# Attention followed by channel mixing: the on-chip decoding of weight pieces, spread differently over three engines

## The chip, the cores and the metric

The kernel runs on one core of a Trainium2 chip. The core has a matrix engine (TensorE, in the profile PE, with its weight loads as PEld), three engines for elementwise work (VectorE or DVE, ScalarE or ACT, GpSimd or POOL), and SyncE (SP), which here issues nearly all transfers. Each engine works through its own instructions in order. The metric is the device time of one execution in microseconds (us). Before the change it is 1101.88 us, the median of 3 runs (1100.26 to 1106.89).

## The reference

The first part is linear attention with random features, for 8 batches of 8 heads, 576 rows and 64 columns; the second is a mixing along the rows by a product of low rank and then a two-layer network over the 512 channels.

```python
def phi(x):                                  # q and k scaled first
    h = np.einsum('bhsd,md->bhsm', x, omega) - np.sum(x * x, axis=-1, keepdims=True) / 2.0
    return np.exp(h - np.max(h, axis=-1, keepdims=True)) / np.sqrt(m)
kv = np.einsum('bhsm,bhsd->bhmd', phi(k), v)
num = np.einsum('bhsm,bhmd->bhsd', phi(q), kv)
den = np.einsum('bhsm,bhm->bhs', phi(q), np.sum(phi(k), axis=2))[..., None] + 1e-06
x = (num / den)                              # heads side by side: 8 x 576 x 512
...
h = x.transpose(0, 2, 1) @ U @ V             # U 576 x 32, V 32 x 576
u = x + h.transpose(0, 2, 1)
out = u + np.maximum(u @ w_ch1, 0.0) @ w_ch2 # w_ch1 512 x 2048, w_ch2 2048 x 512
```

q, k, v and omega are fp32. U, V, w_ch1 and w_ch2 come in fp64, which the chip has no arithmetic for: the kernel reads each number as two 32-bit words and builds an fp32 number from them. fp32 products are made on TensorE from a high and a low part of each operand.

## The kernel before, in words

**Attention.** 16 units (a pair of heads each, keys or queries of them) of 9 tiles of 128 rows make 144 steps; the loop at L761 to L843 writes them out with fixed delays between the stages of one step (the table `DELAY`). A step's chain is: load of kt or qt (SP, L531), transposition xT (VectorE, L551), high part xh (ScalarE, L555), low part xl (GpSimd, L559), the projection p_p (TensorE, three products, L678 to L680), the negative maximum nm over its features (VectorE, L686), four exponentials e, one for each 128x128 quarter (ScalarE, L693), and then, for keys, p_kv (TensorE, L590), and for queries a transposition p_q (TensorE, L616), its copy eT (ScalarE or VectorE, L621), the product p_n (TensorE, L636) and the division into x (VectorE, L661). "Exp step 30" below means the four exponentials of the thirtieth step.

**Mixing.** As soon as a pair of batches has its x, a generator (`mixing`, 4 pairs, 9 tiles each) makes a high part mh (ScalarE, L347) and a low part ml (L349) of each 128x512 tile of x, multiplies them by U and V, and stores u. The low part is made on GpSimd, and on VectorE for the last pair.

**Decoding.** In two of three steps the loop advances the generator `decoding` by one slot. A piece is 128x512 numbers of a weight. It is loaded as 128x1024 words (SP, L183) into one of two raw buffers. For the first 11 pieces (U, two of V, eight of w_ch1, `EARLY`), the ones that the attention loop finishes, the work is: absolute value of the high word as a float (ScalarE, L132); on VectorE a clamp to two bounds (L150), a shift (L151), the merge of the sign from the raw high word (L154), a mask that keeps the exponent (L157) and the low word times that exponent (L158), which is the last to read the raw buffer; and on GpSimd one addition (L172). These are five slots, one VectorE step each. Pieces after that have three slots: for them ScalarE also casts the low word to an integer (L135) and the addition is one of integers. The ScalarE steps of the next piece are written in the fourth slot (third for later pieces), and the next load in the last.

**What sets the order.** The instructions are handed to a scheduler that simulates the engines with costs of its own and orders each engine's instructions by that; those wrapped in `K`, that is `tc.keep_in_program_order`, keep the order in which they are written. SP issues its transfers in the order that results, and a transfer into a buffer that is still in use holds up all transfers behind it.

After attention comes an opening, then the up phase (`unit`, L855, products L891) and the down phase (L1181, L1200); the remaining pieces are decoded there.

## Time and profile before

| | before |
|---|---|
| median of 3 runs | 1101.88 us |
| the profiled execution | 1101.12 us, span 1099.3 us |
| mean granted TensorE clock | 0.979 |
| PE, PEld busy | 95%, 93% of the span |
| DVE, ACT, POOL busy | 78%, 55%, 47% |
| the attention loop | about the first 325 us |

A row of the windows view gives a stretch of the execution, its length, the busy time of each engine with the number of its instructions, and the granted clock. A row of the waits view names an engine and a line that stood idle and what ended that idleness: total, times, longest. A row of the timeline gives start, length, engine, line and operation, and in brackets the idle time ahead of it with what ended it. A row of the groups view gives count, total busy time, mean of one in ns, and after the bar the idle time before them.

### The profile page before, as it was taken

How to read it: one execution, taken by the hardware profiler on the slowest of the kernel's cores; microseconds unless marked ns; L12 is line 12 of the kernel's file. 1: busy time of each engine (PE TensorE's matmuls, PEld its weight loads, DVE VectorE, ACT ScalarE, POOL GpSimd, SP SyncE). 2: the span in 40 equal slices, each digit the busy share in tenths (PEclk: the TensorE clock that was granted, in tenths of full speed). 3: DMA queues.
4: the chain of work that ended last, by engine and by line, in shares of the span. 5: the costliest groups of instructions: out<-in, count | busy, mean ns of one | idle time of the engine just before them, and what ended most of it. 6: DMA issues, size and time to landing. Idle time of an engine off the chain costs nothing. (4 is left out here: it accounts for less than half of the span.)

```text
span 1099.3 us, 23900 instructions
## 1 busy us (share of the span) xinstructions
PE 1049.2 (95%) x8497; PEld 1023.6 (93%) x8497; DVE 857.2 (78%) x1550; ACT 601.1 (55%) x1471; POOL 520.9 (47%) x451
## 2 busy tenths in 40 slices
PE   8999988999997899999999999989999999999998
PEld 7998878899996899899999999979999999999998
DVE  3787998898898778766665555778888888888886
ACT  4877978889873555555453344554443443344433
POOL 3445976956433534313312102545456455564563
PEclk8898999999997999999999999999999999999999
DMA  7778577576434686778778743544544444444442
GB/s 129 138 143 168 96 175 154 104 181 120 92 87 102 200 226 133 193 208 215 212 192 213 202 124 107 164 121 154 172 159 145 168 159 144 165 162 172 156 144 97
DMA packets 382199, 170.31 MB, mean 155 GB/s; under 512 B 283488, under 2 KB 357216, under 8 KB 377472
## 3 DMA queue, kind: packets, MB, share of 16 engines
q1 hardware_dynamic: 382016, 168.72, 58.5%
q8 instruction: 67, 1.10, 0.4%
q14 instruction: 52, 0.43, 0.1%
q0 software_dynamic: 64, 0.07, 0.0%
HBM read 107.91 MB, written 60.82 MB: 153 GB/s over the span
## 5 line engine op out<-in xcount | busy, mean ns | idle before, releaser
L1054 ACT CAST gh<-gs 128x512 fp32r<-128x512 f32 x140 | 83.2, 619 | 208.1 <-DVE gs L1028 161.0
L693 ACT ACTIVATE e<-p_p,nm 128x128 f32<-128x128 f32 x576 | 166.8, 389 | 27.6 <-DVE nm L686 20.5
L1028 POOL TENSOR_TENSOR gs<-graw 128x512 f32<-128x512 f32 x70 | 113.3, 1639 | 110.9 <-DMA graw<-g 79.4
L559 POOL TENSOR_TENSOR xl<-xT,xh 128x384 fp32r<-128x384 f32 x96 | 101.6, 1076 | 116.9 <-ACT xh L555 92.9
L875 ACT ACTIVATE g<-g 128x512 f32<-128x512 f32 x108 | 67.8, 631 | 161.2 <-DVE g L879 116.8
L1055 DVE TENSOR_TENSOR gl<-gs,gh 128x512 fp32r<-128x512 f32 x140 | 112.5, 815 | 53.5 <-ACT gh L1054 53.5
L686 DVE TENSOR_REDUCE nm<-p_p 128x4 f32<-128x512 f32 x144 | 98.1, 682 | 28.5 <-PE p_p L680 14.8
L1126 POOL TENSOR_TENSOR u<-u,p 128x256 f32<-128x256 f32 x72 | 80.4, 1146 | 55.4 <-DVE u L1126 54.2
L678 PE MATMUL p_p<-omh,xh 128*128 128x256 f32 x288 | 94.6, 329 | 2.3 <-ACT e L693 2.2
L172 POOL TENSOR_TENSOR wf<-wf,low 128x512 int32<-128x512 int32 x24 | 32.1, 1337 | 113.2 <-ACT g L875 59.9
L636 PE MATMUL p_n<-kv,eT 128*128 128x65 f32 x512 | 76.3, 278 | 7.6 <-ACT eT L621 3.4
L680 PE MATMUL p_p<-omh,xl 128*128 128x256 f32 x288 | 83.1, 289 | 0.0
L679 PE MATMUL p_p<-oml,xh 128*128 128x256 f32 x288 | 82.6, 287 | 0.0
L891 PE MATMUL p_n<-uh,wh 128*128 128x256 f32 x272 | 78.6, 289 | 3.9 <-DVE g L879 3.9
L636 PEld LDWEIGHTS p_n<-kv,eT 128*128 128x128 f32 x512 | 70.1, 199 | 13.0 <-DVE eT L621 4.0
L1200 PE MATMUL p_p<-wh,gh 128*128 128x256 f32 x288 | 81.1, 282 | 0.0
L1200 PE MATMUL p_p<-wh,gl 128*128 128x256 f32 x288 | 81.0, 281 | 0.0
L1200 PE MATMUL p_p<-wl,gh 128*128 128x256 f32 x288 | 80.9, 281 | 0.0
L1055 DVE TENSOR_TENSOR gl<-graw,gh 128x512 fp32r<-128x512 f32 x107 | 75.2, 730 | 4.4 <-ACT gh L1054 4.4
L1200 PE MATMUL p_q<-wh,gl 128*128 128x256 f32 x276 | 77.8, 282 | 0.7 <-DVE gl L1055 0.6
L891 PE MATMUL p_n<-uh,wl 128*128 128x256 f32 x272 | 78.2, 287 | 0.0
L891 PE MATMUL p_n<-ul,wh 128*128 128x256 f32 x272 | 78.1, 287 | 0.0
(246 smaller groups left out, 4055.6 us busy)
## 6 DMA issues: line engine op xcount, KB each, us to landing
g<-g SPq DMA_DIRECT2D x288, 128.0 KB, 2.4
graw<-g SPq DMA_DIRECT2D x36, 1024.0 KB, 5.0
raw<-in_moe_w_ch_dram SPq DMA_DIRECT2D x22, 512.0 KB, 4.7
u_dram<-ut SPq DMA_DIRECT2D x36, 256.0 KB, 2.4
uraw<-u_dram SPq DMA_DIRECT2D x144, 64.0 KB, 2.6
u<-u_dram SPq DMA_DIRECT2D x36, 256.0 KB, 2.6
out_dram<-u SPq DMA_DIRECT2D x36, 256.0 KB, 2.2
kt<-in_k_dram SPq DMA_DIRECT2D x120, 72.0 KB, 2.6
```

The source lines that it names most:

```text
L559: nc.gpsimd.tensor_tensor(out=self.xl[-1], in0=self.turned, in1=f32(self.xh[-1]), op=ALU.subtract)
L636: nc.tensor.matmul(pn[:, h, :], eT[:, h, :], kv[:, h, s // 5, :], start=True, stop=True)
L678: nc.tensor.matmul(o, part.xh[g][:, ts], oh, start=True, stop=False)
L679: nc.tensor.matmul(o, part.xh[g][:, ts], ol, start=False, stop=False)
L680: nc.tensor.matmul(o, part.xl[g][:, ts], oh, start=False, stop=True)
L686: nc.vector.tensor_reduce(out=self.nm[:, :n], in_=self.pp[:, :n], axis=AX.X, op=ALU.max, negate=True)
L693: nc.scalar.activation(out=self.e[:, j, :], in_=self.pp[:, j, :], func=AF.Exp, bias=self.nm[:, j : j + 1])
L891: K(nc.tensor.matmul(p[:, f, :], x[:, k, fs], y[:, k, :], start=first, stop=(k == 1 and y is ul), skip_group_check=True,))
L1028: K(engine.tensor_tensor(out=to, in0=self.val[x], in1=self.val[y], op=op))
L1054: K(nc.scalar.copy(out=h, in_=v))
L1055: K(nc.vector.tensor_tensor(out=l, in0=v, in1=f32(h), op=ALU.subtract))
L1200: K(nc.tensor.matmul(acc[bank][:, half, :], x[:, ks], y[:, f, :], start=(now.s == 0 and k == 0 and half == 0 and x is h and y is wh), stop ...
```

## The change

All pieces are now decoded as the later ones were: ScalarE casts the low word (L134 in the new numbering, directly behind the absolute value, L132) and GpSimd adds integers (L166), so the mask and the low word's product leave VectorE. For the first 11 pieces the clamp moves from VectorE to GpSimd as well (L139), so VectorE has a shift (L150) and a sign merge (L153) left. The slots of these pieces remain five, with work in the second and the third only. GpSimd's addition and the next load are written in the third slot, since the sign merge is now the last reader of the raw high word; the ScalarE steps of the next piece are written in the fifth. In the mixing, the low parts of odd tiles go to VectorE for the first three pairs too: 12 of their 27.

```diff
         def magnitude(i):
             if i < len(jobs):
-                mags[i] = jobs[i][2]()
-                nc.scalar.activation(out=mags[i], in_=f32(raws[i][:, :, 1]), func=AF.Abs)
-                if i >= lean:
-                    lows[i] = dec.tile([P, PIECE], I32, name="low", tag="de", bufs=2)[:, : jobs[i][1]]
-                    nc.scalar.activation(out=lows[i], in_=raws[i][:, :, 0], func=AF.Copy, scale=2.0**-29)
+                m = mags[i] = jobs[i][2]()
+                nc.scalar.activation(out=m, in_=f32(raws[i][:, :, 1]), func=AF.Abs)
+                lows[i] = dec.tile([P, PIECE], I32, name="low", bufs=2)[:, : jobs[i][1]]
+                nc.scalar.activation(out=lows[i], in_=raws[i][:, :, 0], func=AF.Copy, scale=2.0**-29)
+                if i < early:
+                    bound(nc.gpsimd, m)
+
+        def bound(engine, m):
+            return engine.tensor_scalar(m, m, _LEAST, _MOST, ALU.max, ALU.min)
...
             slots = [
-                lambda: nc.vector.tensor_scalar(m, m, _LEAST, _MOST, ALU.max, ALU.min),
+                lambda: bound(nc.vector, m),
...
-                lambda: nc.vector.tensor_scalar(words(e), words(m), 0xFF800000, None, ALU.bitwise_and),
-                lambda: nc.vector.scalar_tensor_tensor(e, low, 2.0**-52, e, ALU.mult, ALU.mult),
             ]
-            if i >= lean:
-                slots = slots[:3]
+            if i < early:
+                slots = [lambda: None, *slots[1:], lambda: None, lambda: None]
             for j, slot in enumerate(slots):
-                tc.keep_in_program_order(slot())
+                op = slot()
+                if op is not None:
+                    K(op)
                 for _ in range(-(-len(rest) // (len(slots) - j))):
                     rest.pop(0)()
-                if j == (len(slots) - 1 if i >= lean else 3):
+                if j == 2:
+                    K(nc.gpsimd.tensor_tensor(out=m.bitcast(I32), in0=m.bitcast(I32), in1=low, op=ALU.add))
+                    fetch(i + 1 + depth())
+                if j == len(slots) - 1:
                     magnitude(i + 1)
-                if j == len(slots) - 1:
-                    fetch(i + 1 + depth())
                 yield
-            whole = (lambda ap: ap.bitcast(I32)) if i >= lean else (lambda ap: ap)
-            nc.gpsimd.tensor_tensor(out=whole(m), in0=whole(m), in1=e, op=ALU.add)
             rest = [lambda fn=fn, m=m: fn(m) for fn in job[3:]]
...
-                rest = nc.vector if last else nc.gpsimd
+                rest = nc.vector if last or t % 2 else nc.gpsimd
                 rest.tensor_tensor(out=xl, in0=x[:, t, :], in1=f32(xh), op=ALU.subtract)
```

The scheduler's order is changed in the whole attention loop. Two places show how. The first is SP's queue around the loads of the fifth and the sixth piece (both of w_ch1); vt and vm are loads of v, kt and qt those of k and q. Before:

```order
L531 DMA kt_976<-in_k_dram 32x18x32 x8
L531 DMA qt_1014<-in_q_dram 32x18x32 x8
L573 DMA vt1_122<-in_v_dram 128x4x64 x2
L577 DMA vm1_123<-in_v_dram 64x2x64
L183 DMA raw_1123<-in_moe_w_ch1_dram 128x1024
L573 DMA vt1_122<-in_v_dram 128x4x64 x2
L577 DMA vm1_123<-in_v_dram 64x2x64
L531 DMA kt_1288<-in_k_dram 32x18x32 x8
L531 DMA qt_1326<-in_q_dram 32x18x32 x8
L183 DMA raw_1372<-in_moe_w_ch1_dram 128x1024
```

The same stretch of SP's queue after the change, where these two loads are raw_1024 and raw_1259:

```order
L529 DMA kt_975<-in_k_dram 32x18x32 x8
L529 DMA qt_1013<-in_q_dram 32x18x32 x8
L181 DMA raw_1024<-in_moe_w_ch1_dram 128x1024
L571 DMA vt1_122<-in_v_dram 128x4x64 x2
L575 DMA vm1_123<-in_v_dram 64x2x64
L571 DMA vt1_122<-in_v_dram 128x4x64 x2
L575 DMA vm1_123<-in_v_dram 64x2x64
L529 DMA kt_1289<-in_k_dram 32x18x32 x4
L181 DMA raw_1259<-in_moe_w_ch1_dram 128x1024
L529 DMA kt_1289<-in_k_dram 32x18x32 x4
L529 DMA qt_1327<-in_q_dram 32x18x32 x8
```

The fifth load has moved ahead of three transfers, two of vt and one of vm; the sixth ahead of twelve, four of kt and eight of qt. In the same way the third load (the second piece of V) has moved ahead of three transfers and the fourth (the first of w_ch1) ahead of six.

The second place is ScalarE where it first reads the fifth piece, between exp steps 30 and 33 (e_1189, e_1222, e_1254 and e_1284). Before:

```order
L693 ACTIVATE e_1189<-p_p_1146,nm_1187 128x128 x4
L621 COPY eT_1194<-p_q_1175 128x256
L322 CAST svm_119<-sv_118 128x64
L555 CAST xh_1206<-xT_1192 128x384
L555 CAST xh_1236<-xT_1196 128x384
L693 ACTIVATE e_1222<-p_p_1178,nm_1220 128x128 x4
L693 ACTIVATE e_1254<-p_p_1211,nm_1252 128x128 x4
L621 COPY eT_1260<-p_q_1240 128x256
L693 ACTIVATE e_1284<-p_p_1243,nm_1282 128x128 x4
L132 ACTIVATE wf_1059<-raw_1123 128x512
L555 CAST xh_1307<-xT_1297 128x384
```

The same exp steps on ScalarE after the change (e_1187, e_1220, e_1252 and e_1285):

```order
L691 ACTIVATE e_1187<-p_p_1147,nm_1185 128x128 x2
L553 CAST xh_1204<-xT_1190 128x384
L132 ACTIVATE wf_1121<-raw_1024 128x512
L134 ACTIVATE low_1371<-raw_1024 128x512
L553 CAST xh_1234<-xT_1194 128x384
L691 ACTIVATE e_1220<-p_p_1176,nm_1218 128x128 x4
L691 ACTIVATE e_1252<-p_p_1209,nm_1250 128x128 x4
L619 COPY eT_1261<-p_q_1238 128x256
L691 ACTIVATE e_1285<-p_p_1241,nm_1283 128x128 x4
L553 CAST xh_1308<-xT_1298 128x384
L132 ACTIVATE wf_1652<-raw_1259 128x512
```

ScalarE's first reading of the fifth piece has moved from behind exp step 33 to behind exp step 30, and behind exp step 33 it now reads the sixth.

Counted in the same way for all loads of the loop that wait for a raw buffer (load 3 is the second piece of V, load 4 the first of w_ch1), with the exp step behind which ScalarE first reads it, and the steps that lie between the instruction that frees its raw buffer on VectorE and that reading:

| load | 3 | 4 | 5 | 6 | 7 | 8 | 9 | 10 | 11 | 12 | 13 | 14 |
|---|---|---|---|---|---|---|---|---|---|---|---|---|
| first read behind exp step, before | 20 | 27 | 33 | 38 | 45 | 54 | 59 | 66 | 75 | 84 | 89 | 93 |
| after | 18 | 24 | 30 | 33 | 42 | 48 | 56 | 63 | 72 | 78 | 86 | 95 |
| steps from the freeing to the reading, before | 7 | 7 | 5 | 3 | 2 | 4 | 1 | 1 | 2 | 4 | 1 | 1 |
| after | 6 | 7 | 5 | 1 | 2 | 1 | 1 | 1 | 2 | 1 | 1 | 3 |

More of the change, by code (lines that the diff above doesn't have):

```diff
@@ L114, in raw_place, with decoding @@
         return dec.tile([P, PIECE, 2], U32, name="raw", bufs=RB)
-    def decoding(jobs, late, lean, base):
+    def decoding(jobs, late, early, base):
         raws, mags, lows = {}, {}, {}
@@ L142, in decoding @@
         for i, job in enumerate(jobs):
-            n = job[1]
-            raw, m = raws.pop(i), mags.pop(i)
-            low, high = raw[:, :, 0], raw[:, :, 1]
-            e = lows.pop(i) if i in lows else dec.tile([P, PIECE], F32, name="de", bufs=2)[:, :n]
+            high, m, low = raws.pop(i)[:, :, 1], mags.pop(i), lows.pop(i)
             slots = [
-                lambda: nc.vector.tensor_scalar(m, m, _LEAST, _MOST, ALU.max, ALU.min),
+                lambda: bound(nc.vector, m),
                 lambda: nc.vector.tensor_scalar(
```

## The prediction

> **What bounds the kernel now.** I read the page first: which engine is full.
>
> ```profile
> span 1099.3 us, 23900 instructions
> PE 1049.2 (95%) x8497; PEld 1023.6 (93%) x8497; DVE 857.2 (78%) x1550; ACT 601.1 (55%) x1471; POOL 520.9 (47%) x451
> ```
>
> TensorE is busy 95%, so over the whole run only 50 us are open. Nearly everything that the change touches lies in the attention loop, so I cut that into three stretches in the windows view (start:end, length, busy of PE, PEld, DVE, ACT, POOL, granted clock, DMA share, GB/s).
>
> ```profile
> 25.00:100.00 75.00, 69.32 (x547) 67.13 (x546) 58.88 (x149) 58.60 (x197) 31.54 (x31) 0.91 0.77 147
> 100.00:225.00 125.00, 113.49 (x890) 103.85 (x888) 113.85 (x260) 104.44 (x333) 102.65 (x102) 1.00 0.66 137
> 225.00:325.00 100.00, 99.86 (x848) 96.77 (x848) 89.28 (x226) 86.42 (x281) 45.61 (x46) 1.00 0.57 123
> ```
>
> TensorE runs 848 products per 100 us at the end of the loop, 890 in 125 us in the middle. There VectorE is busy 113.85 of 125 us, ScalarE 104.44, GpSimd 102.65. Next the waits of 0 to 325 us (total, times, longest).
>
> ```profile
> ACT wf L132 <- DMA raw<-in_moe_w_ch_dram: 14.2, 8, 3.6
> PE p_q L616 <- ACT e L693: 7.5, 6, 2.0
> PE p_n L636 <- ACT eT L621: 3.4, 2, 2.7
> ```
>
> ScalarE stands 14.2 us before raw pieces that have not landed. It works in order, so exponentials and copies stand behind them, and TensorE waits 7.5 + 3.4 = 10.9 us for those. The timeline puts nearly all of these idles just behind raw waits, so I count 10.9/14.2 = 0.77 us of end time for a us of raw wait. These are ScalarE's first readings of loads 4 to 14, each with its wait in brackets.
>
> ```profile
> 70.00 0.66 ACT L132 ACTIVATE wf<-raw 128x512 f32<-128x512 f32 x1 [1.57 <-DMA raw<-in_moe_w_ch_dram]
> 83.59 0.66 ACT L132 ACTIVATE wf<-raw 128x512 f32<-128x512 f32 x1 [2.82 <-DMA raw<-in_moe_w_ch_dram]
> 95.69 0.68 ACT L132 ACTIVATE wf<-raw 128x512 f32<-128x512 f32 x1 [0.41 <-DMA raw<-in_moe_w_ch_dram]
> 109.72 0.67 ACT L132 ACTIVATE wf<-raw 128x512 f32<-128x512 f32 x1 [0.45 <-DMA raw<-in_moe_w_ch_dram]
> 131.78 0.72 ACT L132 ACTIVATE wf<-raw 128x512 f32<-128x512 f32 x1
> 145.32 0.66 ACT L132 ACTIVATE wf<-raw 128x512 f32<-128x512 f32 x1 [3.62 <-DMA raw<-in_moe_w_ch_dram]
> 161.89 0.67 ACT L132 ACTIVATE wf<-raw 128x512 f32<-128x512 f32 x1 [0.97 <-DMA raw<-in_moe_w_ch_dram]
> 181.22 0.66 ACT L132 ACTIVATE wf<-raw 128x512 f32<-128x512 f32 x1 [1.47 <-DMA raw<-in_moe_w_ch_dram]
> 201.51 0.73 ACT L132 ACTIVATE wf<-raw 128x512 f32<-128x512 f32 x1
> 216.12 0.66 ACT L132 ACTIVATE wf<-raw 128x512 f32<-128x512 f32 x1 [2.85 <-DMA raw<-in_moe_w_ch_dram]
> 225.28 0.81 ACT L135 ACTIVATE low<-raw 128x512 int32<-128x512 uint32 x1
> ```
>
> Set beside the table of steps in the section on the change, they show what one step of distance between freeing and reading is worth. At one step (loads 9, 10, 13, 14) the waits are 3.62, 0.97, 2.85 and 0, mean 1.86. At two (loads 7 and 11) they are 0.45 and 1.47, mean 0.96; at three (load 6) 0.41; at four (loads 8 and 12) none. Loads 4 and 5 have seven and five steps and wait all the same: SP reaches them late.
>
> **The change part by part.** The sum is made against the profiled execution, 1101.12 us (span 1099.3), 0.07% under the median of 1101.88.
>
> *Reading sooner, early loads.* For the fifth load I need SP's queue around it, and ScalarE where exp step 30 ends.
>
> ```profile
> 77.06 0.99 SPq L573 DMA_DIRECT2D vt<-in_v_dram  x2
> ...
> 78.86 0.53 SPq L183 DMA_DIRECT2D raw<-in_moe_w_ch_dram  x1
> ```
>
> ```profile
> 74.55 0.88 ACT L693 ACTIVATE e<-p_p,nm 128x128 f32<-128x128 f32 x3
> ...
> 75.70 0.96 ACT L555 CAST xh<-xT 128x384 fp32r<-128x384 f32 x2
> ```
>
> SP issues without a gap here, so a load gains what the transfers cost that it is moved past: two of vt and one of vm, 78.86 - 77.06 = 1.80 us. The fifth load is then read at the earliest at 83.59 - 1.80 = 81.79. But ScalarE now wants it behind exp step 30, which ended at 74.55 + 0.88 = 75.43; with one xh (0.48) it stands there at 75.9 and waits 5.9 us, not 2.82. After it come the absolute value (0.66), the new cast (0.73, row below) and the work up to the end of exp step 33, which took from 75.9 to 83.59 - 2.82 = 80.77, so 4.9 us. That point is reached at 81.79 + 1.39 + 4.9 = 88.1; before it was 83.59 + 0.66 = 84.25. The loop is **3.8 us late**. Loads 3 and 4 are read sooner too, but the landing of load 5 swallows what they cost. If load 5 takes as long to land as load 4 did (issued at 64.15, read at 70.00: 5.85 us, where load 5 took 83.59 - 78.86 = 4.73), it is 4.9.
>
> ```profile
> 64.15 0.77 SPq L183 DMA_DIRECT2D raw<-in_moe_w_ch_dram  x1
> ```
>
> Load 6 goes from three steps to one: 1.86 for 0.41, times 0.77: **+1.1**. Below, the early part could cost nothing, if ScalarE's delay is taken up by work that other engines had done ahead.
>
> *The middle, raw waits.* By the table, loads 7 to 13 stand after the change at 2, 1, 1, 1, 2, 1, 1 steps: 5 x 1.86 + 2 x 0.96 = 11.2 us, where the rows give 9.4. +1.8 x 0.77 = **+1.4**. The release itself comes two steps sooner, but the reader has been moved up with it; the table holds only the difference.
>
> *The middle, work.* The groups of 100 to 225 us (count, busy, mean ns, idle before):
>
> ```profile
> L686 DVE TENSOR_REDUCE nm<-p_p 128x4 f32<-128x512 f32 x52 | 35.2, 678 | 7.3 <-ACT e L693 3.9 <-PE p_p L680 2.1 <-ACT y L393 0.6
> L349 POOL TENSOR_TENSOR ml<-x,mh 128x512 fp32r<-128x512 f32 x18 | 23.8, 1336 | 1.6 <-ACT mh L347 1.6
> L172 POOL TENSOR_TENSOR wf<-wf,de 128x512 f32<-128x512 f32 x7 | 9.1, 1303 | 0.0
> L150 DVE TENSOR_SCALAR wf<-wf 128x512 f32<-128x512 f32 x7 | 7.8, 1117 | 0.0
> L158 DVE SCALAR_TENSOR_TENSOR de<-raw,de 128x512 f32<-128x512 uint32 x7 | 6.7, 962 | 0.1
> L157 DVE TENSOR_SCALAR de<-wf 128x512 uint32<-128x512 uint32 x7 | 5.2, 747 | 0.0
> L135 ACT ACTIVATE low<-raw 128x512 int32<-128x512 uint32 x2 | 1.5, 730 | 0.0
> ```
>
> The 52 maxima count the steps: 125/52 = 2.40 us a step, and 2.22 without the 9.4 us of raw waits. VectorE's work is 113.85/52 = 2.19 a step: between the raw waits VectorE sets the pace. The change takes three operations of seven pieces from it, 7.8 + 5.2 + 6.7 = 19.7 us, and adds 8 of the 18 low parts (12 of 27 over the loop). Their price on VectorE is in the groups of 225 to 325 us and of the whole run:
>
> ```profile
> L349 DVE TENSOR_TENSOR ml<-x,mh 128x512 fp32r<-128x512 f32 x3 | 2.0, 670 | 0.0
> ...
> L349 DVE TENSOR_TENSOR ml<-x,mh 128x512 fp32r<-128x512 f32 x9 | 8.1, 898 | 0.4 <-ACT mh L347 0.3
> ```
>
> Between 670 and 898 ns I take 800: 6.4 us. VectorE comes to 100.6 us, 1.93 a step. ScalarE gets seven casts of 730 ns, 5.1 us, and comes to 109.6 us, 2.11 a step: it becomes the slowest. What the middle gains is 113.85 - 109.6 = **-4.2 us**, not 13.
>
> The Trainium skill ("SBUF — State Buffer", section "SBUF: two separate sides") says that a VectorE operation with two SBUF inputs and a GpSimd operation that reads SBUF exclude each other for a whole instruction. By that rule each moved low part could stand a GpSimd addition longer (1.30, from L172), 8 x 1.3 = 10.4 us, VectorE would come to 111.0 and the gain to 2.9; the 898 of the second row, against 670, shows part of such a stretch, and the 4.2 stays in my sum.
>
> *GpSimd.* It loses 8 x 1336 ns = 10.7 us and gets seven clamps. No row shows a clamp of this size there. Below it is bounded by a plain fill (335 ns for 260 columns, so 0.66 us for 512), above by an addition with two inputs, 1303.
>
> ```profile
> L732 POOL MEMSET vm<- 128x260 f32 x2 | 0.6, 335 | 0.0
> ```
>
> With 1.0, nearer the middle since it has one input, that is 7 us: 98.9 us, 1.90 a step, below ScalarE. Its cost is put at nothing: it would be on the path only if the clamp took over 2.5 us (11 us more). Behind a clamp that waits for ScalarE stand low parts xl, and those wait for ScalarE's xh behind the same absolute value. VectorE's shift now waits for the clamp, but its slot is steps later than the absolute value.
>
> *After the loop* the code is the same but for the order of the additions. Its lows waited for raw loads and for these additions:
>
> ```profile
> L135 ACT ACTIVATE low<-raw 128x512 int32<-128x512 uint32 x14 | 9.7, 689 | 11.9 <-DMA raw<-in_moe_w_ch_dram 7.3 <-POOL wf L172 4.6
> ```
>
> An addition that comes sooner can save part of 4.6, a load further back in SP's queue can add to 7.3: 0, with 3 either way.
>
> Sum: 3.8 + 1.1 + 1.4 - 4.2 = +2.1, so 1101.1 + 2.1 = **1103 us**. One per cent, 11 us, is about what a measurement of this kernel can tell from no change.
>
> **The rivals.**
>
> *The waits eat everything, 1116 us.* Load latency decides: by the page a raw load lands 4.7 us after its issue,
>
> ```profile
> raw<-in_moe_w_ch_dram SPq DMA_DIRECT2D x22, 512.0 KB, 4.7
> ```
>
> and with the issue's 0.4 that is 5.1 us from freeing to reading. With VectorE no longer behind, a step of distance covers only its 2.1 us: 3.0 us of wait at one step, 0.9 at two. Loads 6 to 13 (six at one step, two at two) then wait 19.8 us instead of 9.8: +10.0 x 0.77 = 7.7. ScalarE's stalls would leave VectorE's saving without use (0 for -4.2), load 5 costs its upper 4.9, and one more stall like that at 85 us costs a dip of the clock:
>
> ```profile
> 85.00:90.00 5.00, 4.61 (x23) 4.61 (x23) 2.08 (x4) 3.00 (x13) 2.92 (x3) 0.50 0.90 137
> ```
>
> half of 5 us, 2.5. Together +15.1. For it speak the 3.62 and 2.85 at one step; against it the 0.97 and 0. It makes the kernel slower by over 1% from 11/0.77 = 14.3 us more raw wait, so 28.5 in place of 14.2. Chance 0.25.
>
> *VectorE was the bound, 1090 us.* If its relief gives the middle the pace of the end of the loop,
>
> ```profile
> L686 DVE TENSOR_REDUCE nm<-p_p 128x4 f32<-128x512 f32 x50 | 34.2, 684 | 6.5 <-PE p_p L680 2.0 <-ACT e L693 1.8 <-ACT eT L621 1.5
> ```
>
> 100/50 = 2.00 a step for 2.22, 52 steps give -11.4, and the raw waits stay as they were. Against it stands ScalarE: 2.11 a step with the casts, 86.42/50 = 1.73 at the end of the loop. Chance 0.16.
>
> *Reading sooner does nothing, 1097 us.* The loads come sooner by as much as their readers, early and in the middle, and only the -4.2 is left. Against it: the fifth load gains 1.8 us where its reader moves by three steps. Chance 0.19.
>
> **How the numbers follow.** My forecast has 0.40. It and its neighbour at 1097 lie within 1%, as does the lower edge of the first rival: 0.60 for no change that can be measured. The faster rival lies on the 1% line, and with some of it below and a little of 1097 I give faster 0.16; slower 0.24 is nearly all of the first rival. The range reaches from 1090, the faster rival, to 1117, the slower one with a us more; below lie those cases in which the casts hide as well, above those in which several pieces stall like load 5.
>
> **What would show it right or wrong.** Right: ScalarE's first reading of load 5 starts near 81.8 with a wait of about 6 us in front of it, and exp step 33 ends near 88; the raw waits of 0 to 325 us come to 19 to 23 us (5.9 + 1.9 + 11.2 and a little at loads 3 and 4); VectorE in the middle falls to about 100 us and ScalarE rises to 110 in a stretch of equal steps; the maxima no longer wait there; L139 on GpSimd means 0.7 to 1.3 us; low parts on VectorE 0.7 to 0.9. Wrong: raw waits below 14 us (the loads gained more than their readers), a step of 2.0 in the middle (ScalarE hides its casts), raw waits over 28, a clamp over 2.5 us on GpSimd, or a change in the up or down phase.

## The result, and the profile after

The changed kernel takes 1109.65 us (median of 20 runs, 1105.60 to 1116.49), the kernel before 1103.94 us (20 runs, 1099.31 to 1106.89). The ratio is 1.0064 with a 95% interval of 1.0047 to 1.0081: 7 us slower by the ratio, 5.7 us between the two medians, less than the 1% that I had called measurable, but with so many runs clear of no change. Two of the runs below, one each of two kernels, ran slow at a granted clock of 0.84 and 0.75, where all others have 0.97 to 0.99, and are left out of the medians and ratios. The profiled execution took 1106.02 us (span 1103.8), near the lower end of its kernel's times.

The page of the changed kernel, and the windows of the three stretches:

```profile
span 1103.8 us, 23863 instructions
...
PE 1053.7 (95%) x8497; PEld 1028.4 (93%) x8497; DVE 855.3 (77%) x1529; ACT 605.9 (55%) x1482; POOL 521.6 (47%) x450
```

```profile
25.00:100.00 75.00, 67.87 (x544) 65.30 (x542) 55.33 (x133) 59.21 (x197) 37.33 (x36) 0.94 0.74 141
100.00:225.00 125.00, 115.60 (x902) 106.57 (x901) 108.06 (x251) 107.39 (x340) 102.05 (x100) 0.99 0.67 135
225.00:325.00 100.00, 99.62 (x842) 96.42 (x841) 91.59 (x229) 86.25 (x281) 41.76 (x41) 1.00 0.58 126
```

VectorE's work in the middle stretch fell from 113.85 to 108.06 us, not to the 100.6 that I had worked out; ScalarE's rose from 104.44 to 107.39; GpSimd's hardly moved. The waits of 0 to 325 us:

```profile
ACT wf L132 <- DMA raw<-in_moe_w_ch_dram: 9.8, 6, 2.9
...
PE p_n L634 <- ACT eT L619: 6.0, 3, 3.0
...
PE p_q L614 <- ACT e L691: 5.7, 8, 1.5
...
ACT low L134 <- DMA raw<-in_moe_w_ch_dram: 1.8, 2, 1.0
```

ScalarE waits 9.8 + 1.8 = 11.6 us for raw pieces, less than the 14.2 before, while I had expected 19 to 23. Yet TensorE waits 6.0 + 5.7 = 11.7 us for ScalarE, more than the 10.9 before. Where it does so, the timeline shows: ScalarE's first readings of loads 4, 5 and 6, and TensorE's waits behind them.

```profile
65.13 0.66 ACT L132 ACTIVATE wf<-raw 128x512 f32<-128x512 f32 x1 [2.41 <-DMA raw<-in_moe_w_ch_dram]
...
79.06 0.69 ACT L132 ACTIVATE wf<-raw 128x512 f32<-128x512 f32 x1 [0.33 <-DMA raw<-in_moe_w_ch_dram]
...
87.00 0.67 ACT L132 ACTIVATE wf<-raw 128x512 f32<-128x512 f32 x1 [1.81 <-DMA raw<-in_moe_w_ch_dram]
```

```profile
67.06 0.32 PE L634 MATMUL p_n<-kv,eT 128*128 128x65 f32 x1 [3.00 <-ACT eT L619]
...
81.02 0.33 PE L614 MATMUL p_q<-ident,e 128*128 128x128 f32 x1 [0.77 <-ACT e L691]
...
88.95 0.33 PE L634 MATMUL p_n<-kv,eT 128*128 128x65 f32 x1 [2.22 <-ACT eT L619]
```

In the kernel before, TensorE's waits behind the readings of loads 4 and 5 were these:

```profile
71.39 0.33 PE L616 MATMUL p_q<-ident,e 128*128 128x128 f32 x1 [1.13 <-ACT e L693]
...
85.39 0.47 PE L636 MATMUL p_n<-kv,eT 128*128 128x65 f32 x1 [2.75 <-ACT eT L621]
```

To see where the time goes I cut the loop at exp steps, at the end of the fourth exponential of steps 22, 42 and 94 (start:end, length, busy of PE, PEld, DVE, ACT, POOL, granted clock, DMA share, GB/s). The cuts are rounded to 0.1 us, so a length can differ by 0.1 from the table further down. Before:

```profile
58.90:103.00 44.10, 39.89 (x323) 38.62 (x322) 36.02 (x93) 33.43 (x112) 18.00 (x18) 0.92 0.83 156
103.00:227.50 124.50, 112.99 (x885) 103.35 (x885) 113.04 (x256) 103.94 (x331) 103.50 (x103) 1.00 0.66 139
```

and after:

```profile
59.00:105.10 46.10, 39.77 (x321) 38.68 (x321) 34.39 (x88) 34.76 (x113) 24.04 (x22) 0.93 0.78 151
105.10:228.90 123.80, 114.40 (x891) 105.36 (x889) 107.58 (x248) 106.24 (x336) 100.08 (x100) 0.99 0.67 137
```

Up to step 22 the two stand level (58.9 and 59.0 us). Steps 22 to 42 take 2.1 us longer, steps 42 to 94 take 0.8 us less, and the rest of the loop is the same within 0.5 us; step 142 ends at 323.8 instead of 322.0 us. From there to the end it is 780.0 us against 777.3. In this pair of profiles the loss is +2.1 in the early part, -0.8 in the middle, +2.7 behind the loop. The early loss is TensorE's idle time: it is as busy as before (39.77 and 39.89 us), and the waits shown above add up to 6.0 us after, 3.9 before, although ScalarE's waits for raw pieces there are hardly different (4.5 and 4.8 us).

Three operations answer for VectorE's and GpSimd's work in the middle (groups of 100 to 225 us):

```profile
L347 POOL TENSOR_TENSOR ml<-x,mh 128x512 fp32r<-128x512 f32 x10 | 13.5, 1347 | 2.3 <-ACT mh L345 2.3
...
L139 POOL TENSOR_SCALAR wf<-wf 128x512 f32<-128x512 f32 x5 | 9.6, 1915 | 3.0 <-PE p_kv L588 1.5 <-ACT wf L132 1.5
...
L347 DVE TENSOR_TENSOR ml<-x,mh 128x512 fp32r<-128x512 f32 x8 | 8.6, 1073 | 0.3 <-ACT mh L345 0.3
L153 DVE SCALAR_TENSOR_TENSOR wf<-raw,wf 128x512 uint32<-128x512 uint32 x8 | 8.5, 1061 | 0.0
```

A clamp on GpSimd takes 1915 ns, above my upper bound of 1303; a low part on VectorE 1073 ns, not 800; the sign merge went from 937 to 1061 ns.

### The profile page after: what moved, and what is told of

Same layout as the page of the kernel before. It is cut to its first block, busy times and chain, and to the rows that moved or that the text cites. A ratio compares the mean times of both kernels' runs of the same rounds, so it can differ in the third digit from the quotient of the medians.

```text
span 1103.8 us, 23863 instructions
## 1 busy us (share of the span) xinstructions
PE 1053.7 (95%) x8497; PEld 1028.4 (93%) x8497; DVE 855.3 (77%) x1529; ACT 605.9 (55%) x1482; POOL 521.6 (47%) x450
## 5 line engine op out<-in xcount | busy, mean ns | idle before, releaser
L166 POOL TENSOR_TENSOR wf<-wf,low 128x512 int32<-128x512 int32 (+2 forms) x35 | 44.9, 1282 | 127.1 <-ACT g L873 65.7
L634 PEld LDWEIGHTS p_n<-kv,eT 128*128 128x128 f32 x512 | 70.6, 200 | 11.6 <-ACT eT L619 6.7
```

The lines of the kernel that those rows point to most:

```text
L634: nc.tensor.matmul(pn[:, h, :], eT[:, h, :], kv[:, h, s // 5, :], start=True, stop=True)
```

## The experiments

Each kernel was timed in five rounds, 5 to 12 runs, beside the kernel before, whose medians were 1101.24 us (first four runs), 1100.87 (next four) and 1102.77 (last four); so the ratios are to be compared, not the times. "Held" means that ScalarE's readings of raw pieces are kept in program order. The last columns are from one profiled execution each: raw waits of ScalarE in the first 325 us (all weights), and the time of exp steps 22 to 42 and 42 to 94.

| kernel | median us | ratio to before, 95% interval | raw waits us | steps 22 to 42 | steps 42 to 94 |
|---|---|---|---|---|---|
| before | | 1 | 14.2 | 44.0 | 124.6 |
| changed | 1109.65 | 1.0064 (1.0047 to 1.0081) | 11.6 | 46.1 | 123.8 |
| changed, readings held | 1097.65 | 0.9972 (0.9950 to 0.9995) | 1.5 | 39.9 | 122.5 |
| changed, no clamp | 1106.45 | 1.0040 (1.0021 to 1.0060) | 9.8 | 46.3 | 124.1 |
| changed, clamp on VectorE | 1106.94 | 1.0054 (1.0028 to 1.0080) | 13.6 | 49.0 | 125.8 |
| changed, low parts on GpSimd | 1110.52 | 1.0087 (1.0056 to 1.0117) | 10.6 | 46.8 | 134.0 |
| before, readings held | 1098.47 | 0.9982 (0.9965 to 0.9998) | 6.5 | 42.9 | 125.2 |
| changed, late additions as before | 1105.80 | 1.0035 (1.0013 to 1.0057) | 11.8 | 48.3 | 124.8 |
| changed, held, late additions as before | 1097.87 | 0.9960 (0.9938 to 0.9982) | 1.9 | 39.9 | 123.8 |
| changed, written later, not held | 1111.64 | 1.0096 (1.0068 to 1.0124) | 11.3 | 46.8 | 122.5 |
| changed, loads 1 to 6 held | 1109.35 | 1.0059 (1.0036 to 1.0082) | 9.5 | 39.9 | 130.9 |
| changed, loads 7 to 11 held | 1106.20 | 1.0030 (1.0005 to 1.0054) | 7.0 | 49.1 | 123.4 |
| before, held and one slot later | 1098.76 | 0.9974 (0.9954 to 0.9993) | 5.6 | 42.7 | 124.5 |
| changed, held, no shift and merge | 1092.86 | 0.9919 (0.9891 to 0.9946) | 1.6 | 40.8 | 118.8 |

### The readings held where they were

My theory was that ScalarE's readings, which the scheduler moves up with the loads, cost what the relief of VectorE brings. The rivals were the clamp with what it stretches, and the part behind the loop.

```diff
-                nc.scalar.activation(out=m, in_=f32(raws[i][:, :, 1]), func=AF.Abs)
+                (K if i < early else lambda op: op)(nc.scalar.activation(out=m, in_=f32(raws[i][:, :, 1]), func=AF.Abs))
...
-                nc.scalar.activation(out=lows[i], in_=raws[i][:, :, 0], func=AF.Copy, scale=2.0**-29)
+                (K if i < early else lambda op: op)(nc.scalar.activation(out=lows[i], in_=raws[i][:, :, 0], func=AF.Copy, scale=2.0**-29))
```

> The changed kernel, with one thing added: the two ScalarE readings of each of the first 11 raw pieces are kept in program order, so that the scheduler no longer moves them up with the loads. The loads keep their places in SP's queue; between the freeing of a buffer and the reading of the next load there are now 8 to 10 exp steps instead of 1 or 2 in the middle, and loads 4 and 5 are read behind exp steps 27 and 33 as in the kernel before. Theory A (the gain is lost to ScalarE standing before raw pieces that have not landed: 9.8 + 1.8 = 11.6 us of it in the profile after, at 0.77 us of end time each): the raw waits of the loop fall below 4 us, and the time falls by 6 to 9 us against the changed kernel, to 1101 to 1104, at or below the kernel before. Theory B (the clamp of 1.9 us on GpSimd and the operations it stretches on VectorE cost the time; raw waits are hidden): 1108 to 1110, as changed. Theory C (the time is lost behind the loop): also 1108 to 1110, with the loop's end some us earlier.

The ratio falls from 1.0064 to 0.9972, by 0.0092 or 10 us, somewhat more than the 6 to 9 expected. The kernel's work is the same; what changes is the order, of the readings first of all, and of some other instructions that the scheduler moves with them. The wait and the two stretches of this kernel:

```profile
ACT wf L132 <- DMA raw<-in_moe_w_ch_dram: 1.5, 1, 1.5
```

```profile
58.50:98.40 39.90, 37.76 (x325) 36.46 (x325) 36.08 (x88) 34.32 (x114) 23.08 (x22) 1.00 0.81 153
98.40:220.80 122.40, 114.30 (x884) 104.70 (x883) 106.99 (x248) 105.81 (x336) 100.95 (x100) 0.99 0.72 145
```

Raw waits are down to 1.5 us, the granted clock in steps 22 to 42 is up from 0.93 to 1.00, and step 142 ends at 315.8 instead of 323.8 us: 6.2 of these 8.0 us are won in steps 22 to 42, 1.3 in steps 42 to 94. The profiled execution itself is this kernel's longest (1105.48 us): it lost 7.5 us behind the loop, against the profile of the changed kernel, and I read only its loop.

### The clamp, left out or moved back

```diff
-                if i < early:
-                    bound(nc.gpsimd, m)
```

> The changed kernel without the clamp of the first 11 pieces: that part of the computation is left out (it bounds the magnitudes before the shift). The order of all else stays nearly as it was: ScalarE reads the loads behind the same exp steps. Theory A: as the changed kernel within 2 us, 1108 to 1111, the raw waits still about 12 us. Theory B: the sign merge (1061 ns) and the low parts on VectorE (1073 ns) of the middle fall to about 800 and 850 ns, VectorE's busy time in the middle from 108 to about 104, and the time by 3 to 6 us, to 1104 to 1107.

```diff
-                if i < early:
-                    bound(nc.gpsimd, m)
...
-                slots = [lambda: None, *slots[1:], lambda: None, lambda: None]
+                slots = [*slots, lambda: None, lambda: None]
```

> The changed kernel with the clamp of the first 11 pieces back on VectorE, in the first of the five slots; all else as changed. Theory A: VectorE in the middle gets seven clamps of 0.8 to 1.1 us, 5 to 8 us more, and is the fullest engine again (about 114 of 125); raw waits hardly change: 1109 to 1114. Theory B: without the 1.9 us operation on GpSimd the other operations on VectorE come down to 0.8 to 0.9 us and pay for it: 1104 to 1108.

Without the clamp 1.0040, with it on VectorE 1.0054; both intervals overlap that of the changed kernel. The sign merge came down to 979 ns without it, not to 800, and VectorE's work in the middle did not fall at all (108.2 us):

```profile
L151 DVE SCALAR_TENSOR_TENSOR wf<-raw,wf 128x512 uint32<-128x512 uint32 x8 | 7.8, 979 | 0.1
```

The long clamp on GpSimd is worth between nothing and 5 us (2.6 by the ratios); it isn't what makes the difference of 10.

### The low parts back on GpSimd

```diff
-                rest = nc.vector if last or t % 2 else nc.gpsimd
+                rest = nc.vector if last else nc.gpsimd
```

> The changed kernel with the mixing's low parts of the first three pairs all back on GpSimd, where they were before; all else as changed. VectorE in the middle loses eight low parts of 1073 ns (108 to about 99.5 us), GpSimd gains eight of 1347 ns (102 to about 113). Theory A: no more than 2 us either way, 1108 to 1112, since ScalarE's waits stay. A third theory (the moved low parts are what costs, because they stand before the maxima on VectorE): 1104 to 1107. If GpSimd becomes the fullest engine at 113 of 125, slower than the changed kernel: 1112 to 1116.

1.0087: not faster, so the moved low parts are not what costs, and slower by 0.0023 with overlapping intervals. Its profiled execution is its slowest (1117.48 us, clock 0.969), so the 134.0 us of its middle say little.

### The kernel before, readings held

```diff
-                nc.scalar.activation(out=mags[i], in_=f32(raws[i][:, :, 1]), func=AF.Abs)
+                (tc.keep_in_program_order if i < lean else lambda op: op)(nc.scalar.activation(out=mags[i], in_=f32(raws[i][:, :, 1]), func=AF.Abs))
```

> The kernel before, with one thing added: ScalarE's absolute value of each of the first 11 raw pieces is kept in program order. SP's queue stays as it was; the readings fall 1 to 5 exp steps later. Between the freeing of a buffer and the reading there are 4 to 6 steps, where there were 1 to 4. Theory A (raw waits cost 0.77 us of end time each us, whatever else the change does): the 14.2 us of raw waits fall below 4 us, since load 5 keeps its reading behind exp step 33, and the time falls by 7 to 10 us against the kernel before, to a ratio of 0.991 to 0.994, which would be faster than the changed kernel with its readings held (0.997): the change's other parts then cost 3 to 6 us. Theory B (VectorE's relief is worth its 4 us once nothing hides it): the ratio comes out at 0.998 to 1.001, slower than the changed kernel held.

The ratio is 0.9982, at the lower edge of theory B's range and far from theory A's. The raw waits fell from 14.2 to 6.5 us, by less than expected, and the time by 2 us; per us of raw wait that is 0.26, where the changed kernel gave 1.0 (10.1 us of time for 10.2 us of waits). But the two figures are not for the same waits. Here mostly the middle's have gone; loads 4 and 5 are read behind exp steps 27 and 33 as before, and ScalarE still stands before them:

```profile
68.54 0.67 ACT L132 ACTIVATE wf<-raw 128x512 f32<-128x512 f32 x1 [1.50 <-DMA raw<-in_moe_w_ch_dram]
...
82.23 0.66 ACT L132 ACTIVATE wf<-raw 128x512 f32<-128x512 f32 x1 [1.30 <-DMA raw<-in_moe_w_ch_dram]
```

The same edit with the reading written one slot later asks again what the middle's waits cost:

```diff
-                if j == (len(slots) - 1 if i >= lean else 3):
+                if j == len(slots) - 1:
                     magnitude(i + 1)
```

> The kernel before with the readings of the first 11 pieces kept in program order and written one slot later. The readings of loads 4 and 5 stay behind exp steps 27 and 33, where they waited 1.57 and 2.82 us; those of loads 6 to 11 move to 41, 51, 57, 63, 72 and 81, so the 9.4 us of raw waits of the middle go. Theory A1: 9.4 x 0.77 = 7.2 us less than the kernel before, ratio 0.993 to 0.995. Theory A2: in the middle the waits stood beside VectorE's work, which sets the pace there; the ratio is 0.997 to 1.000, as with the readings held alone (0.998).

0.9974, with 8.6 us of raw wait less: 2.9 us, 0.33 a us; loads 4 and 5 still waited 1.31 and 1.99 us. In the kernel before, the raw waits of the middle cost next to nothing: its middle with the readings held takes 124.5 to 125.2 us with 2.3 to 3.7 us of them, as long as with 9.4 us (124.6). That is what theory A2 had. What the early waits cost in this kernel no run tells, since none took them away altogether.

### The additions behind the loop

```diff
                 if j == 2:
-                    K(nc.gpsimd.tensor_tensor(out=m.bitcast(I32), in0=m.bitcast(I32), in1=low, op=ALU.add))
+                    if i < early:
+                        K(nc.gpsimd.tensor_tensor(out=m.bitcast(I32), in0=m.bitcast(I32), in1=low, op=ALU.add))
                     fetch(i + 1 + depth())
...
                 yield
+            if i >= early:
+                nc.gpsimd.tensor_tensor(out=m.bitcast(I32), in0=m.bitcast(I32), in1=low, op=ALU.add)
```

> The changed kernel, but for the pieces behind the first 11 GpSimd's addition is written as before, after the third slot and not kept in program order; the attention loop is as changed. In the profiles the changed kernel needs 780.0 us from exp step 142 to the end, the kernel before 777.3. Theory C (what the loop does not explain is this addition's place): the part behind the loop comes back to about 777 us and the ratio to the kernel before falls from 1.0064 to 1.003 to 1.005. If that difference is only the clock and chance: 1.005 to 1.008.

> The changed kernel with the readings of the first 11 pieces held and with the later pieces' additions written as before. If theories A and C both hold, their gains add: 0.997 less 0.002 to 0.003 is 0.994 to 0.996. If only A holds: 0.996 to 0.999, as with the readings held alone.

1.0035 against 1.0064, and with the readings held 0.9960 against 0.9972. Both go the way of theory C, by 0.0029 and 0.0012, and in both pairs the intervals overlap: 1 to 3 us are possible, not shown. The profiles can't show it either: the part behind step 142 took 777.3, 781.4 and 779.0 us in the kernel before and its two held forms, though its code is the same there, 780.0 and 787.5 in the changed kernel and its held form, and 778.5 and 779.1 in the two kernels of this edit. The kernel with both edits has the lowest ratio of those that compute everything, 0.9960 (0.9938 to 0.9982), below both kernels of the change, and is not told apart from the one with the readings held alone.

### Written later, but not held

```diff
-                    fetch(i + 1 + depth())
-                if j == len(slots) - 1:
+                if j == (3 if i < early else 2):
                     magnitude(i + 1)
+                if j == len(slots) - 1:
+                    fetch(i + 1 + depth())
```

> The changed kernel with the next load written in the last of five slots and ScalarE's readings in the fourth, as in the kernel before: the reading of raw buffers sooner is undone, the rest of the change stays, and the readings are not held. In its order loads 5, 6 and 7 are read behind exp steps 31, 36 and 45 (changed: 30, 33 and 42; before: 33, 38 and 45). Theory A: there is still 9 to 15 us of raw wait, because the scheduler again puts the readings one or two steps behind the freeing, and the ratio stays at 1.004 to 1.008. If it is the sooner loads that drag the readings ahead of what has landed: raw waits below 8 us and a ratio of 0.999 to 1.003.

1.0096 and 11.3 us of raw wait, as theory A had it for the waits, and a little above its ratio.

```profile
ACT wf L132 <- DMA raw<-in_moe_w_ch_dram: 8.7, 5, 2.9
...
ACT low L134 <- DMA raw<-in_moe_w_ch_dram: 2.6, 2, 2.0
```

Writing the load and the reading where they were written before didn't help, as long as the scheduler might move them.

### Early readings held, late readings held

```diff
-                (K if i < early else lambda op: op)(nc.scalar.activation(out=m, in_=f32(raws[i][:, :, 1]), func=AF.Abs))
+                (K if i < min(early, 6) else lambda op: op)(nc.scalar.activation(out=m, in_=f32(raws[i][:, :, 1]), func=AF.Abs))
...
```

> The changed kernel with the ScalarE readings of loads 1 to 6 alone kept in program order; loads 7 to 11 are read as in the changed kernel, one or two steps behind the freeing. In the profiles the changed kernel has 4.5 us of raw wait in the first 100 us and 7.1 from 100 to 225. Exp steps 22 to 42 took 46.1 us there and 39.9 with all readings held; steps 42 to 94 took 123.8 and 122.4. Theory A1 (each us of raw wait costs 0.77 us wherever it stands): the first waits are worth 3.5 us of the 10, ratio to the kernel before 1.002 to 1.004. Theory A2 (the first waits cost more than their length, because TensorE then stands long enough for its clock to be halved, and those of the middle are hidden): steps 22 to 42 fall to 40 to 41 us at a clock near 1.0 and the ratio to 0.997 to 1.000.

```diff
-                (K if i < early else lambda op: op)(nc.scalar.activation(out=m, in_=f32(raws[i][:, :, 1]), func=AF.Abs))
+                (K if 6 <= i < early else lambda op: op)(nc.scalar.activation(out=m, in_=f32(raws[i][:, :, 1]), func=AF.Abs))
...
```

> The changed kernel with the ScalarE readings of loads 7 to 11 alone kept in program order; loads 3 to 6 are read behind exp steps 18, 24, 30 and 33 as in the changed kernel. The raw waits of the middle go, those of the first 100 us stay. Theory A1: 7.1 x 0.77 = 5.5 us less than the changed kernel, ratio 1.001 to 1.002. Theory A2: steps 22 to 42 still take 45 to 47 us, and the ratio stays at 1.004 to 1.007.

The first went as theory A2 said in the stretch that it changes, 39.9 us at a clock of 1.00, and not in the ratio: 1.0059. What steps 22 to 42 gained, steps 42 to 94 gave back.

```profile
57.90:97.80 39.90, 37.80 (x325) 36.50 (x325) 36.09 (x88) 34.34 (x113) 23.06 (x22) 1.00 0.84 156
97.80:228.70 130.90, 118.25 (x885) 108.87 (x884) 106.63 (x248) 106.60 (x336) 100.50 (x100) 0.95 0.65 135
```

At load 7, the first reading that is not held, ScalarE arrives 7.3 us sooner than in the changed kernel (97.8 for 105.1), and the reading can start only 3.8 us sooner (102.31 for 106.06):

```profile
102.31 0.66 ACT L132 ACTIVATE wf<-raw 128x512 f32<-128x512 f32 x1 [4.52 <-DMA raw<-in_moe_w_ch_dram]
```

```profile
104.66 0.35 PE L614 MATMUL p_q<-ident,e 128*128 128x128 f32 x1 [4.88 <-ACT e L691]
```

In the changed kernel that wait was 0.97. With only the later readings held the ratio is 1.0030: 4.6 us less raw wait, 3.7 us less time, between the theories (its early part, untouched, took 49.1 us in its profile). Holding one half gives 0.0005 or 0.0034, holding both 0.0092: the wait that was taken away early came back at the next reading, which still stands one or two steps behind its load's freeing. These two ratios don't refute theory A1, a fixed price for each wait wherever it stands: for the 2.1 and 4.6 us of raw wait that really went, 0.77 a us gives 1.0049 and 1.0032, both inside the measured intervals. What speaks against it are the two held forms of the kernel before, where it gives 0.9946 and 0.9940, below both intervals, and the stretches. In the table steps 22 to 42 take 39.9 us in the three kernels that have no raw wait there (readings held, held with late additions as before, loads 1 to 6 held). They take 42.7 to 44.0 us in the kernel before and its held forms, with 2.8 to 4.8 us of it, and 46.1 to 49.1 in the changed kernel and its forms whose early readings are not held, with 3.5 to 6.5 us. The middle shows no such order, but for the 4.52 us at load 7 here, behind which TensorE stood 4.88.

### No shift and no merge

```diff
-                slots = [lambda: None, *slots[1:], lambda: None, lambda: None]
+                slots = [lambda: None] * 5
```

> The changed kernel with all readings held, and for the first 11 pieces the shift and the sign merge on VectorE are left out (the weights are then built wrongly from their words). VectorE loses seven times 0.6 and 1.2 us in the middle, 109 to about 96.5 us. If VectorE still sets the pace of the middle once no raw wait is left: steps 42 to 94 fall from 122.4 to 110 to 115 us and the ratio to the kernel before to 0.984 to 0.990. If the chain of one step or another engine sets it: 118 to 122 us and 0.993 to 0.997.

```profile
99.40:218.20 118.80, 112.93 (x893) 104.39 (x891) 99.30 (x237) 105.60 (x337) 96.06 (x98) 1.00 0.71 148
```

Steps 42 to 94 take 118.8 us instead of 122.5, with 7.7 us less of VectorE's work (106.99 to 99.30); the ratio is 0.9919, between the two expectations. VectorE still takes part in setting the pace once the raw waits are gone, at about half a us a us in this pair of profiles, but it doesn't set it alone. Part of the 3.7 us may be the granted clock (1.00 here, 0.99 with the merge), and the chain of a piece is shorter too, which this run doesn't keep apart from VectorE's work. What holds the middle at 2.3 us a step, while VectorE, ScalarE and GpSimd have a tenth to a fifth of their time free, isn't settled.

## Why the prediction was right or wrong

The forecast of 1103 us was too low by 6.65; the time lies in the range, and no change by over 1% was right. Against the kernel before I had worked out +2.1 us, and 7 were measured (5.7 between the medians). That the time lies in the range is in good part luck. By my own signs the mechanism failed: the raw waits came to 11.6 us, below the 14 that I had named as wrong. One must not add up the terms as if they had been right: most were not.

**The fifth load.** I had 3.8 us for it, from a landing at 81.79 and a ScalarE that arrives at 75.9. It landed for a reading at 79.06, and ScalarE arrived at 78.7, so the wait was 0.33, not 5.9. The step that failed is "SP issues without a gap here, so a load gains what the transfers cost that it is moved past". The load was issued not at 77.06 but here:

```profile
73.98 0.43 SPq L181 DMA_DIRECT2D raw<-in_moe_w_ch_dram  x1
```

The sixteen loads of k and q ahead of it, which took 6.33 + 5.52 us before, took 4.33 + 4.22. The rows show no gap, but before the change three single issues among them took 0.90, 2.25 and 1.61 us where most take 0.50; what held them isn't shown. And "the landing of load 5 swallows what they cost" was wrong for load 4: its wait, 2.41 us, stopped TensorE for 3.00, as load 5's had stopped it for 2.75 before. The mechanism, a reader that goes further ahead than its load, was right one load sooner: ScalarE stood before load 4 5.7 us sooner than in the kernel before (62.7 for 68.4) and could read it 4.9 us sooner (65.1 for 70.0). At load 5 it was the other way round: ScalarE came 2.0 us sooner, and the reading could start 4.5 us sooner. That exp step 33 ended 4.0 us late (84.8 for 80.8, not near 88) and step 34 3.5 us late (89.9 for 86.4), close to my 3.8, is luck; by step 42 2.1 us of it are left. For load 6, three steps before and one after, I had 1.86 us; it is 1.81.

**Raw waits in the middle.** 11.2 us were forecast, 5.3 + 1.8 = 7.1 measured. The mean wait of 1.86 at one step of distance doesn't carry over from one order to another; at the same distances the rows of the middle went from 9.4 to 7.1 us. One reading that fits is that a lag early in the loop gives the loads time: where I took that lag away (loads 1 to 6 held), the middle had 9.5 us of raw wait.

**The price, 0.77 us for a us of raw wait.** This is the step that mattered most. It put TensorE's waits for ScalarE down to the raw waits one by one, wherever they stand. Measured over whole kernels, it is 0.26 and 0.33 for the waits that holding took away in the kernel before, most of them in the middle, and 1.0 for those in the changed kernel, early and middle. By the stretches of the profiles it goes by place: in the changed kernel 4.5 us of early raw wait went with 6.2 us of time (46.1 to 39.9), and 5.6 us of the middle's with 1.3. Holding the later readings alone gave 3.7 us by the ratio, but the two intervals allow anything from near nothing to 7, so the price of the middle's waits in the changed kernel isn't settled.

What is shown is that the place of the readings decides: holding them gives 0.0092 in the changed kernel and 0.0018 in the kernel before. The loads come sooner after the change, and held readings find the early ones landed; where the scheduler moves the readings up with the loads, the raw wait of the early part stays (4.5 us for 4.8). Why about the same raw wait stops TensorE 2.1 us longer there, and so why the changed kernel is slower and not merely as slow, stays open. That VectorE's backlog hid the waits of the middle before is a reading that fits (113 us of work in 124.5 there, 107 after), but no run took only that backlog away, and by the profiles the middle of the changed kernel hides most of them too; it stays argued.

**VectorE's relief.** I had it fall to 100.6 us and the middle gain 4.2. It fell to 108.06 (1073 ns for a moved low part, 1061 for a sign merge, and one step more in the window), and the middle gained 0.8 us as it stood, of the 4.2, at a granted clock of 0.99 for 1.00. With the readings held in both kernels the changed kernel is ahead by 0.0010 to 0.0014 (0.9972 and 0.9960 against 0.9982 and 0.9974), with overlapping intervals, and the held kernel before still has early raw waits that the held changed one has not; so these ratios don't tell what the relief is worth. By the profiles the middle with readings held is 122.5 and 123.8 us against 125.2 and 124.5: 0.7 to 2.7 us. The rule from the Trainium skill ("SBUF — State Buffer", section "SBUF: two separate sides") that I had set beside it, of a shared port that a GpSimd operation and a VectorE operation with two SBUF inputs hold in turn, gave 2.9 (and 111.0 us of work) and was the nearer: both operations that grew have two SBUF inputs. For each moved low part it would have meant 0.8 + 1.3 = 2.1 us, which was too high (1073 ns).

**GpSimd.** The clamp's 1.0 us should have been 1.9, but it was under the 2.5 us from which I had said that it would decide, and leaving it out gave 2.6 us (1.0040 for 1.0064), with overlapping intervals. The cost of nothing isn't refuted, but the duration under it was wrong, above the upper bound of 1303 that I had taken.

**Behind the loop.** 0 with 3 either way; 2.7 us in one pair of profiles, which is within what this part varies by, and 1 to 3 by the two runs, not shown. No run shows that the addition kept in order saved anything.

**The rivals.** "The waits eat everything" was the nearest: slower, through ScalarE before raw pieces, with VectorE's saving nearly unused. But its mark, raw waits over 28 us, never came, nor did its 1116; the loss came with 11.6 us of raw waits, fewer than before. The rival at 1090, that VectorE sets the pace of the middle, fell: with no raw waits and 7.7 us less of VectorE's work the middle still takes 2.28 us a step, not 2.00. "Reading sooner does nothing", at 1097, fell with the time, which rose, and with the first experiment, in which the place of the readings was worth 10 us.

## What to carry to other kernels

When an edit lets a transfer start sooner, look at where the scheduler puts its reader: count the steps between the freeing of the buffer and the first reading, on the engine that reads, before and after; if they don't grow, the reader has moved up with the load and the earlier start may buy nothing, and pinning the reader may be worth more than the edit (here 10 us for two pinned instructions a piece). A total of waits has no fixed price: take the waits away one stretch at a time and in both kernels, and check which ones went, since here the early ones of the changed kernel cost more than their length and the later ones of the kernel before next to nothing. And a row of queue time without a gap doesn't show that the queue could not have been faster.

## What the runs showed of the hardware

**A clamp on GpSimd is slow, and not because of neighbours.** An operation of one tensor with two scalars took 1170 to 1920 ns on GpSimd for sizes from 288 to 512 columns. At 512 columns the mean is 1916 ns from 25 to 100 us and 1915 from 100 to 225 us, although VectorE is busy 74% of the one stretch and 86% of the other; an addition of two tensors of the same size took 1278. On VectorE the same instruction takes 421 ns in the median, and up to 1253 in the loop. The Trainium skill ("GPSIMD Engine Reference", section "Elementwise — side-by-side cycle accounting") gives 769 ns for 512 elements as the measured best case of a tight loop, and has two inputs as what makes an addition slower; here the operation with a single input is the slower by half.

```profile
L139 DVE TENSOR_SCALAR wf<-wf x24: 385/421/1253, 215.7 to 590.5; 128x512 f32<-128x512 f32 x24
L139 POOL TENSOR_SCALAR wf<-wf x11: 1170/1915/1920, 35.9 to 177.2; 128x512 f32<-128x512 f32 x8, 128x288 f32<-128x288 f32 x2, 128x320 f32<-128x320 f32 x1
```

**The clock fell after idles of 1.4 and 2.1 us.** At 14 us, long before the change can act, TensorE stood 2.11 us in the profile of the changed kernel and then ran at half clock for over 10 us (rows of the idle and of the windows; the granted clock is the third number from the end):

```profile
14.01 0.33 PE L588 MATMUL p_kv<-vt,e 128*128 128x65 f32 x1 [2.11 <-DMA vt<-in_v_dram]
```

```profile
15.00:20.00 5.00, 5.00 (x25) 5.00 (x25) 2.03 (x4) 2.19 (x7) 0.96 (x2) 0.50 0.72 145
20.00:25.00 5.00, 5.00 (x25) 5.00 (x25) 0.99 (x2) 2.29 (x8) 0.99 (x2) 0.50 0.81 130
```

In the profile of the kernel before TensorE stood 1.39 us at the same place, and the clock fell there too, for a shorter time:

```profile
15.00:20.00 5.00, 5.00 (x32) 5.00 (x31) 2.33 (x4) 3.33 (x11) 1.89 (x2) 0.63 0.74 149
20.00:25.00 5.00, 5.00 (x32) 5.00 (x32) 1.87 (x3) 1.69 (x7) 0.06 (x1) 0.69 0.67 107
```

After an idle of 2.02 us at 146 us in the same profile it stayed at 1.00, so the length of one idle alone doesn't decide. Step 10 ended 3.0 us later in the changed kernel, and by step 22 the two were level again. The Trainium skill ("TensorE: Matmul & The Clock Gate", Part 1) has the clock halved after one idle window of some 3.4 us, a window that runs free of the kernel; the idles here are shorter, so the measurement decides against the length, and the free-running window would explain why the same few us of idle cost one execution more than another, which no run here tests. The 20 times of the changed kernel lie 11 us apart, which is more than the whole effect; a single profile of this kernel tells where waits stand, and only several that agree tell what they cost.
